# Dealing the residues of g by chunk over VectorE's two places, and issuing the adding transfers in the quarter unit of their squares

## The chip, the core and the metric

The kernel runs on one core of a Trainium2 chip. The metric is the device time in microseconds (us) of one execution; the median of three is given. The engines are TensorE (PE; its weight loads are shown as PEld), VectorE (DVE), ScalarE (ACT), GpSimd (POOL) and SyncE (SP). POOL and SP issue the transfers here, and the core's 16 DMA engines carry them.

## The reference

```python
qn = q / (np.linalg.norm(q, axis=1, keepdims=True) + 1e-06)   # q, k, v: (4, 6080, 256) float32
kn = k / (np.linalg.norm(k, axis=1, keepdims=True) + 1e-06)
s = kn.transpose(0, 2, 1) @ qn / tau                          # 256 x 256 for each of 4 batches
a = np.exp(s - s.max(-1, keepdims=True)); a /= a.sum(-1, keepdims=True) + 1e-09
x = (v @ a).reshape(24320, 256)
h = x @ w_in                                                  # 256 x 2048
g = np.where(h > 0.0, h, np.exp(np.minimum(h, 0.0)) - 1.0)
return g @ w_out                                              # 2048 x 256
```

A channel attention over tokens is followed by a feed-forward layer with ELU. Everything is float32. To keep its accuracy on TensorE, a number is split into a high part, rounded to the shorter type fp32r, and a residue, the rest of it, also in fp32r; one product is then three matmuls (high by high, high by residue, residue by high).

## The kernel before

The attention matrix of a batch is multiplied into w_in first, so that for each batch a 256 x 2048 matrix stands for both. Tokens are dealt into 48 chunks of 512 or 496, 12 to a batch. The first batch is computed in plain steps, up to about 592 us of the profile. The other 36 chunks are computed in 18 pairs, and a pair in 8 units (4 quarters fq of the 2048 columns, by j = 0 and 1): 144 units, numbered u from 0. A unit computes a 2 x 2 block of h (two chunks x = 0 and 1, two rows of columns, row = 0 and 1) with seven products in place of eight (the scheme of Strassen and Winograd), each of three matmuls (L1146, into bank_a, bank_e and bank_b), and sums of them on VectorE (L1576, L1591). The four results go through ELU: ScalarE relu and exp (L1220, L1221), VectorE the maximum (`largest`, L1224) into a tile e (named held or other). I call these four by row and chunk: e11 is row 0, x 0; e12 row 0, x 1; e21 row 1, x 0; e22 row 1, x 1.

Each e is then split. `hi_part` lets POOL issue a transfer (L1238) that rounds e into a tile of high parts (t or g), in the unit of its own. `lo_parts` subtracts it from e on VectorE in the next unit (L1245, out is a tile of residues g); it is called at two places of that unit, `before[0]` (behind L1576) and `before[1]` (behind the maximum of e21). The products with w_out (L1156 to L1158, into po) take row 1 in the second half of the next unit, x 0 ahead of x 1, and row 0 in the first half of the unit after it. In most units POOL issues the parts in the order e11, e21, e22, e12. In the unit with fq = 0 and j = 1 of every pair but the first, called the turn (u = 9, 17, 25, ...), ScalarE copies out finished sums first, and the order is e11, e21, e12, e22.

Beside the units, other work is dealt in by a planner. A task has an engine, a cost, tasks it waits for, and a due time or a level; `spend(engine, budget, now)` is called at fixed places of a unit, and writes there what is ready. Time is counted in quarters of a unit (`now = 4 * u`, and up to `now + 3`). What is written sets each engine's order, and engines then run through their orders with semaphores; the planner's times are no clock. In levels below 2 any ready task may go; in 2 and 3 only the first of the queue.

The tasks of `plan_rows` prepare the attention of the next batch (2 and then 3) from 24 groups of rows of q and k. For a group: SP loads q and k into a raw tile (`load`, L1364); POOL rounds them straight from memory (`hi`, L1375; ScalarE does it for the last group, L1373); VectorE makes the residues (`lo`, L1351); ScalarE squares the raw tile in place (L1381); POOL adds the squares into acc by an accumulating transfer (`add`, L1384). There are two raw tiles, so the load of group g waits for the adds of group g - 2. A number `late` is the count of quarters that must lie between a task and those it waits for on other engines. After the last group `plan_soft` follows (norms, softmax, transposes), and `plan_s` makes the seven matrices of the products for the next batch.

Of the kernel before, what the change touches and what calls it, by code (L numbers as in the profile page):

```python
# [54 lines left out]
def channel_attention_then_elu_ffn(ctx: ExitStack, tc, q, k, vT, tau, w_in, w_out, outT):  # L55
# [905 lines left out]
    done = []  # L961
# [5 lines left out]
    ACT, DVE, POOL, PE, SP = "act", "dve", "pool", "pe", "sp"  # L967
# [90 lines left out]
    def columns(p):  # L1058
        return span(NB + 2 * p)[1:]
# [47 lines left out]
    x = s1 - 13  # L1107
# [129 lines left out]
        else:  # L1237
            nc.gpsimd.dma_start(hi, e)  # L1238

    def lo_parts(u, row):  # L1240
        n = columns(units[u][0])[1]
        for x in range(2):
            quads[u, row, x].append(lo_ring.pop(0))
            e, hi, lo = (y[:, 0:n] for y in quads[u, row, x])
            nc.vector.tensor_sub(lo, e, hi.bitcast(F32))  # L1245
            e_ring.append(quads[u, row, x][0])
# [82 lines left out]
    def plan_rows(b, t):  # L1329

        prior = state["s_prior"]
        last_gram = None
        slots = {}
        added = {}

        def raw_of(g, y):
            x = (2 * g + y) % 4
            if x not in slots:
                room = work.tile([P, 2, 2, C], F32, tag="raw", bufs=5, name=f"raw_{b}_{x}")
                slots.update({x: room[:, 0], x + 1: room[:, 1], ("tile", x): room})  # L1340
            return slots[x]

        for g in range(NG):
            n = min(2, RP - 2 * g)
            before = state["gram_tasks"][-2 * KT : -KT][-1:] if g >= 2 else [prior.get("lo" if g else "lo before")]
            done, ready, squares = [], [], []

            def lo(g=g):
                hl = state[b, "hl", g]
                raw = slots["tile", 2 * g % 4]  # L1350
                nc.vector.tensor_sub(hl[:, 1], raw, hl[:, 0].bitcast(F32))  # L1351

            def new_hl(g=g):
                state[b, "hl", g] = work.tile([P, 2, 2, 2, C], F32R, tag="qk", bufs=3, name="qk")

            for y in range(2):
                src = (q, k)[y][b]
                rows_of = src[0 : RP * P, :].rearrange("(p r) c -> p r c", r=RP)[:, 2 * g : 2 * g + n, :]

                def load(g=g, n=n, y=y, src=src, rows_of=rows_of):  # L1360
                    raw = raw_of(g, y)
                    if n < 2:
                        nc.gpsimd.memset(raw[:, 1, :], 0.0)
                    nc.sync.dma_start(raw[:, 0:n, :], rows_of)  # L1364
                    if n < 2:
                        nc.sync.dma_start(raw[0:LEFT, 1, :], src[RP * P : N, :])

                def hi(g=g, n=n, y=y, rows_of=rows_of, new_hl=new_hl):
                    if y == 0:
                        new_hl()  # L1370
                    to = state[b, "hl", g][:, 0, y]
                    if n < 2:
                        nc.scalar.copy(to, raw_of(g, y))  # L1373
                    else:
                        nc.gpsimd.dma_start(to, rows_of)  # L1375

                def square(g=g, y=y):
                    if g == 0 and y == 0:
                        state[b, "acc"] = new_acc(b)
                    raw = raw_of(g, y)  # L1380
                    nc.scalar.activation(raw if g else state[b, "acc"][:, y], raw, AF.Square)  # L1381

                def add(g=g, y=y):
                    nc.gpsimd.dma_start(state[b, "acc"][:, y], raw_of(g, y), accum_op=ALU.add)  # L1384

                when = t + PACE * g + y * PACE / 2
                x = task(SP, 0, load, [added[g - 2, y]] if g >= 2 else [prior.get("lo")], when=when, level=2, late=2 if n == 2 else 4)
                if n == 2:
                    h = task(POOL, 0.55, hi, [*before, *done], when=when, level=2, late=1)
                else:  # L1390
                    h = task(ACT, 0.57, hi, [x, *before, *done], when=when, due=t + 16 + 5 * g, late=3)
                done = [h]
                ready += [h, x]
                squares.append((square, add))

            los = [task(DVE, 1.22, lo, ready, due=t + 4 + 4.8 * g, late=3 if n == 2 else 0)]
            for y, (square, add) in enumerate(squares):
                s = task(ACT, 0.57, square, [*los, *([] if g else [prior.get("pw")])], due=t + 4 + 4.8 * g, late=0)
                added[g, y] = task(POOL, 0.55, add, [s, *([(added[g - 1, y], 3)] if g else [])], level=1, late=1) if g else s

            for ct in range(KT):

                def items(g=g, ct=ct):
                    if g == 0 and ct == 0:
                        state[b, "gram"] = ps.tile([P, KT, C], F32, tag="gram", bufs=KT, name=f"gram_{b}")
                    return gram_items(state[b, "hl", g], state[b, "gram"], ct, g == 0, g == NG - 1)

                last_gram = task(PE, 0, items, los, level=2, late=1)
                state["gram_tasks"].append(last_gram)
        return last_gram, [added[NG - 1, y] for y in range(2)]  # L1410
# [142 lines left out]
    before = None  # L1553
    for u, (p, fq, j) in enumerate(units):
        now = PERIOD * u
        c = NB + 2 * p
        b = c // NB
        n = span(c)[2]
        more_room(u)
        if (fq, j) == (0, 0):  # L1560
            plan_pair(p)
        spend(SP, 1, now)
        assert (b, fq) in s_ready, (b, fq, u)
        va, vb, ve, vp = (x[:, 0:n] for x in (bank_a, bank_b, bank_e, p7))

        turn = u > 1 and (fq, j) == (0, 1)
        product(bank_a, p, fq, j, "A11", "B11", True)
        nc.scalar.copy(vb, va)  # L1568
        used = spend(DVE, 2.7, now)
        spend(POOL, 3.9, now)  # L1570
        product(bank_e, p, fq, j, "S3", "T3", True)
        nc.scalar.copy(vp, ve)
        multiply_out(1, now)
        spend(ACT, -0.3 if turn else 1.1, now)
        product(bank_b, p, fq, j, "S2", "T2")
        nc.vector.tensor_add(ve, vb, vp)  # L1576
        if before is not None:
            before[0]()
        product(bank_a, p, fq, j, "A12", "B21")
        e11 = new_quad(u, 0, 0)  # L1580
        relu_exp(e11, va)
        multiply_out(1, now + 1)
        spend(SP, 1, now + 1)
        product(bank_e, p, fq, j, "A22", "T4")
        e21 = new_quad(u, 1, 0)
        relu_exp(e21, ve)
        spend(ACT, -0.3, now + 1)
        largest(e11, va)
        hi_part(u, 0, 0)
        product(bank_b, p, fq, j, "S1", "T1")  # L1590
        nc.vector.tensor_add(vp, vb, vp)  # L1591
        multiply_out(2, now + 1)
        spend(ACT, -0.3 if turn else 0.3, now + 2)
        if not turn:
            e22 = new_quad(u, 1, 1)
            relu_exp(e22, vp)
        largest(e21, ve)
        hi_part(u, 1, 0)
        if before is not None:
            before[1]()  # L1600
        product(bank_b, p, fq, j, "S4", "B22")
        e12 = new_quad(u, 0, 1)
        relu_exp(e12, vb)
        if turn:
            e22 = new_quad(u, 1, 1)
            relu_exp(e22, vp)
        multiply_out(2, now + 2)
        if not turn:
            largest(e22, vp)
            hi_part(u, 1, 1)  # L1610
        multiply_out(2, now + 3)
        largest(e12, vb)
        hi_part(u, 0, 1)
        if turn:
            largest(e22, vp)
            hi_part(u, 1, 1)
        spend(POOL, 4.5, now + 3)
        spend(SP, 1, now + 3)
        used += spend(DVE, min(0.3, 3.0 - used), now + 3)
        spend(ACT, 0.6 if turn else 1.7, now + 3)  # L1620

        before = (lambda u=u: lo_parts(u, 1), lambda u=u: lo_parts(u, 0))

        for row in (1, 0):
            for x in range(2):
                for dt in range(DT):
                    outs.append(
                        (
                            c + x,
                            4 * fq + (1 - row) * 2 + j,  # L1630
                            (u, row, x),
                            dt,
                            (fq, j, row) == (0, 0, 1),
                            (fq, j, row) == (FQ - 1, 1, 0),
                        )
                    )

    now = PERIOD * len(units)
# [41 lines left out]
```

## Time and profile before

| | |
|---|---|
| median of 3 runs | 2103.23 us (2102.28 to 2105.74) |
| the profiled execution | 2105.84 us, span 2104.1 us |
| TensorE clock granted | 1.00 |
| PE, PEld busy | 2076.5 us (99%), 1836.6 us (87%) |
| DVE, ACT, POOL busy | 1589.7 us (76%), 1445.4 us (69%), 484.9 us (23%) |
| DMA | 349.29 MB, mean 166 GB/s |

The span is that of the instructions; the execution's own time is 1.7 us longer. A row of the timeline reads: start, duration, engine, line, operation, out<-in, count, and in brackets the idle time of the engine before it with what ended it. A row of the waits reads: engine and line, what it waited for, us in total, times, longest. DMA issues show as DMA_DIRECT2D on POOL, and on SPq, SyncE's queue.

### The profile page before, as it was taken

How to read it: one execution, taken by the hardware profiler on the slowest of the kernel's cores; microseconds unless marked ns; L12 is line 12 of the kernel's file. 1: busy time of each engine (PE TensorE's matmuls, PEld its weight loads, DVE VectorE, ACT ScalarE, POOL GpSimd, SP SyncE). 2: the span in 40 equal slices, each digit the busy share in tenths (PEclk: the TensorE clock that was granted, in tenths of full speed). 3: DMA queues.
4: the chain of work that ended last, by engine and by line, in shares of the span. 5: the costliest groups of instructions: out<-in, count | busy, mean ns of one | idle time of the engine just before them, and what ended most of it. 6: DMA issues, size and time to landing. Idle time of an engine off the chain costs nothing.

```text
span 2104.1 us, 29468 instructions
## 1 busy us (share of the span) xinstructions
PE 2076.5 (99%) x10009; PEld 1836.6 (87%) x10009; DVE 1589.7 (76%) x2498; ACT 1445.4 (69%) x2428; POOL 484.9 (23%) x853
## 2 busy tenths in 40 slices
PE   9999999999999999999999999999999999999998
PEld 8888888899888888888898888888888888888898
DVE  6988777777887777678688777767878767767675
ACT  6887776677776676667666667666766666666675
POOL 0000000000024343432222343443222222222221
PEclk9999999999999999999999999999999999999999
DMA  9320222221368998964567799996565543543533
GB/s 357 121 81 21 74 77 70 65 70 58 110 192 223 263 238 248 257 175 151 171 189 222 195 258 257 244 256 179 177 189 177 172 154 117 166 155 115 166 122 112
DMA packets 179863, 349.29 MB, mean 166 GB/s; under 512 B 19584, under 2 KB 56320, under 8 KB 178176
## 3 DMA queue, kind: packets, MB, share of 16 engines
q0 software_dynamic: 120960, 228.36, 38.5%
q1 hardware_dynamic: 58608, 118.91, 16.8%
q8 instruction: 79, 1.29, 0.3%
q14 instruction: 72, 0.59, 0.1%
q10 hardware_dynamic: 144, 0.13, 0.0%
HBM read 134.33 MB, written 31.20 MB: 79 GB/s over the span
## 4 chain that ended last, share of the span: by engine, by line
PE 90%; DMA 3%; DVE 3%; ACT 2%; issue 1%; POOL 0%; SPq 0%; DVEq 0%; POOLq 0%; ACTq 0%
PE bank_b L1146 12%; PE po L1157 11%; PE po L1158 11%; PE po L1156 11%; PE bank_e L1146 8%; PE bank_a L1146 8%; PE ph L446 4%; PE ph L444 4%; PE ph L445 4%; PE po L488 4%; PE po L486 4%; PE po L484 4%; PE gram L223 3%; PE gram L572 2%; DMA t<-other 2%
## 5 line engine op out<-in xcount | busy, mean ns | idle before, releaser
L1158 PE MATMUL po<-g,wo 128*128 128x512 f32 (+1 forms) x1158 | 437.6, 378 | 0.0
L1157 PE MATMUL po<-t,wo 128*128 128x512 f32 (+1 forms) x792 | 299.8, 379 | 0.0
L1156 PE MATMUL po<-t,wo 128*128 128x512 f32 (+1 forms) x792 | 299.0, 378 | 0.0
L1576 DVE TENSOR_TENSOR bank_e<-bank_b,p 128x512 f32<-128x512 f32 (+1 forms) x144 | 99.7, 693 | 245.8 <-PE bank_b L1146 238.7
L1158 PEld LDWEIGHTS po<-g,wo 128*128 128x128 f32 x1158 | 218.9, 189 | 28.2
L1568 ACT COPY bank_b<-bank_a 128x512 f32<-128x512 f32 (+1 forms) x144 | 81.5, 566 | 231.6 <-PE bank_a L1146 221.6
L1221 ACT ACTIVATE other<-other 128x512 f32<-128x512 f32 (+1 forms) x325 | 203.7, 627 | 10.3
L1238 POOL DMA_DIRECT2D t<-other x217 | 114.7, 529 | 414.0 <-DVE other L1224 249.2
L1146 PE MATMUL bank_b<-t,s 128*128 128x512 f32 (+1 forms) x528 | 181.6, 378 | 6.1 <-DVE p L1591 5.0
L1156 PEld LDWEIGHTS po<-t,wo 128*128 128x128 f32 x792 | 149.7, 189 | 19.4
L1157 PEld LDWEIGHTS po<-t,wo 128*128 128x128 f32 x792 | 149.8, 189 | 18.8
L115 DVE TENSOR_TENSOR g<-e,g 128x512 fp32r<-128x512 f32 (+1 forms) x192 | 130.9, 682 | 45.8 <-ACT g L114 44.4
L114 ACT CAST g<-e 128x512 fp32r<-128x512 f32 (+1 forms) x192 | 116.7, 608 | 69.4 <-DVE e L461 38.3
L1221 ACT ACTIVATE held<-held 128x512 f32<-128x512 f32 (+1 forms) x251 | 157.6, 628 | 8.0
L1245 DVE TENSOR_TENSOR g<-other,t 128x512 fp32r<-128x512 f32 (+1 forms) x217 | 144.5, 679 | 17.0 <-DMA t<-other 17.0
L223 PE MATMUL gram<-qk 128*128 128x256 f32 x576 | 157.3, 273 | 0.0
L1238 POOL DMA_DIRECT2D t<-held x179 | 94.7, 529 | 224.7 <-DVE held L1224 113.0
L488 PE MATMUL po<-g,wo 128*128 128x512 f32 (+1 forms) x378 | 142.7, 377 | 0.0
L486 PE MATMUL po<-g,wo 128*128 128x512 f32 (+1 forms) x378 | 142.6, 377 | 0.0
L484 PE MATMUL po<-g,wo 128*128 128x512 f32 (+1 forms) x378 | 142.6, 377 | 0.0
L1157 PE MATMUL po<-g,wo 128*128 128x512 f32 (+1 forms) x366 | 138.3, 378 | 0.0
L1156 PE MATMUL po<-g,wo 128*128 128x512 f32 (+1 forms) x366 | 138.1, 377 | 0.0
(282 smaller groups left out, 5503.2 us busy)
## 6 DMA issues: line engine op xcount, KB each, us to landing
t<-other POOLq DMA_DIRECT2D x144, 256.0 KB, 2.3
t<-held POOLq DMA_DIRECT2D x120, 256.0 KB, 2.4
acc<-raw POOLq DMA_DIRECT2D x92, 256.0 KB, 4.7
raw<-in_q_dram SPq DMA_DIRECT2D x76, 256.0 KB, 4.2
raw<-in_k_dram SPq DMA_DIRECT2D x76, 256.0 KB, 4.0
g<-other POOLq DMA_DIRECT2D x72, 256.0 KB, 2.5
t<-other POOLq DMA_DIRECT2D x73, 248.0 KB, 2.2
t<-held POOLq DMA_DIRECT2D x59, 248.0 KB, 2.2
```

The costliest lines, as they stand in the source:

```text
L115: nc.vector.tensor_sub(lo, src, hi.bitcast(F32))
L223: yield nc.tensor.matmul(gram[:, ct, :], hl[:, x, 1, r, cs], in_turns(hl[:, y, 0, r, :]), start=(first and ct == 0 and r == 0 and k == 0), ...
L484: nc.tensor.matmul(o, wo[:, f, 0, ds], hi, start=first(c, f), stop=False)
L486: nc.tensor.matmul(o, wo[:, f, 1, ds], hi, start=False, stop=False)
L488: nc.tensor.matmul(o, wo[:, f, 0, ds], lo, start=False, stop=last(c, f))
L1146: nc.tensor.matmul(bank[:, 0:n], w[:, x], y, start=(begin and k == 0), stop=(k == 2), skip_group_check=True)
L1156: yield nc.tensor.matmul(o, wo[:, f, 0, ds], hi, start=begin, stop=False)
L1157: yield nc.tensor.matmul(o, wo[:, f, 1, ds], hi, start=False, stop=False)
L1158: yield nc.tensor.matmul(o, wo[:, f, 0, ds], lo, start=False, stop=end)
L1221: nc.scalar.activation(e, e, AF.Exp, scale=-1.0)
L1238: nc.gpsimd.dma_start(hi, e)
L1245: nc.vector.tensor_sub(lo, e, hi.bitcast(F32))
```

## The change

There are three parts. First, `lo_parts` is called by chunk in place of by row: at `before[0]` VectorE now makes the residues of e21 and e11, at `before[1]` those of e22 and e12. Second, the `add` tasks get level 3 in place of 1 (behind the other tasks of POOL, and in their order), `late` 0 in place of 1, and the first call of `spend` for POOL in a unit stands behind that for ScalarE; an add can so be written in the quarter of its squares. Third, ScalarE's `hi` of the last group waits 5 quarters after its load in place of 3.

```diff
-    def lo_parts(u, row):
+    def lo_parts(u, x):
         n = columns(units[u][0])[1]
-        for x in range(2):
+        for row in (1, 0):
             quads[u, row, x].append(lo_ring.pop(0))
...
-                    h = task(ACT, 0.57, hi, [x, *before, *done], when=when, due=t + 16 + 5 * g, late=3)
+                    h = task(ACT, 0.57, hi, [x, *before, *done], when=when, due=t + 16 + 5 * g, late=5)
...
-                added[g, y] = task(POOL, 0.55, add, [s, *([(added[g - 1, y], 3)] if g else [])], level=1, late=1) if g else s
+                added[g, y] = task(POOL, 0.55, add, [s, *([(added[g - 1, y], 3)] if g else [])], level=3, late=0) if g else s
...
         used = spend(DVE, 2.7, now)
-        spend(POOL, 3.9, now)
         product(bank_e, p, fq, j, "S3", "T3", True)
         nc.scalar.copy(vp, ve)
         multiply_out(1, now)
         spend(ACT, -0.3 if turn else 1.1, now)
+        spend(POOL, 3.9, now)
...
-        before = (lambda u=u: lo_parts(u, 1), lambda u=u: lo_parts(u, 0))
+        before = (lambda u=u: lo_parts(u, 0), lambda u=u: lo_parts(u, 1))
```

VectorE in unit 98, the one behind the turn of unit 97, before. The two L1245 under L1576 are e21 and e22, the two further down e11 and e12.

```order
L1576 TENSOR_TENSOR bank_e<-bank_b,p_5100 128x512 [waits PE_49,Activation_49]
L1245 TENSOR_TENSOR g_5108<-held,g_5177 128x512 [waits DMASW4_49]
L1245 TENSOR_TENSOR g_5108<-other_5102,t_5107 128x512 [waits DMASW6_49]
L1224 SCALAR_TENSOR_TENSOR other_5103<-other_5103,bank_a 128x512 [waits Activation_49]
L1591 TENSOR_TENSOR p_5100<-bank_b,p_5100 128x512 [waits DVE_49,PE_49]
L1224 SCALAR_TENSOR_TENSOR held<-held,bank_e 128x512 [waits Activation_49]
L1245 TENSOR_TENSOR g_5108<-other_5104,g_5177 128x512 [waits DMASW3_49]
L1245 TENSOR_TENSOR g_5108<-held,t_5107 128x512 [waits DMASW5_49,PE_49]
```

The same place now: e21 and e11, and further down e22 and e12.

```order
L1576 TENSOR_TENSOR bank_e<-bank_b,p_5100 128x512 [waits PE_49,Activation_49]
L1245 TENSOR_TENSOR g_5108<-held,g_5177 128x512 [waits DMASW6_49,DVE_49]
L1245 TENSOR_TENSOR g_5108<-other_5104,g_5177 128x512 [waits DMASW5_49,DVE_49]
L1224 SCALAR_TENSOR_TENSOR other_5103<-other_5103,bank_a 128x512 [waits Activation_49]
L1591 TENSOR_TENSOR p_5100<-bank_b,p_5100 128x512 [waits DVE_49,PE_49]
L1224 SCALAR_TENSOR_TENSOR held<-held,bank_e 128x512 [waits Activation_49]
L1245 TENSOR_TENSOR g_5108<-held,t_5107 128x512 [waits DMASW0_49]
L1245 TENSOR_TENSOR g_5108<-other_5102,t_5107 128x512 [waits DMASW7_49,PE_49]
```

Of e22, whose transfer the turn issues last, the subtraction has moved from ahead of L1224 and L1591 to behind them; the count is the same.

POOL from unit 10 into unit 11, before (L1084 are parts of the next pair, from v).

```order
L1084 DMA t_5047<-in_v_dram 128x512 [waits DMAHW4_49,DMAHW3_49,DMASW6_49]
L1238 DMA t_5107<-other_5104 128x512 [waits DMASW7_49,DVE_49,PE_49]
L1238 DMA t_5107<-held 128x512 [waits DMASW0_49,DVE_49,PE_49]
L1238 DMA g_5177<-other_5103 128x512 [waits DMASW1_49,DMASW3_49,DVE_49,PE_49]
L1238 DMA t_5107<-held 128x512 [waits DMASW2_49,DMASW5_49,DVE_49,PE_49]
L1084 DMA s_5105<-in_v_dram 128x512
L1084 DMA t_5047<-in_v_dram 128x512 [waits DMASW4_49]
L1384 DMA acc_5268<-raw_2_5205 128x512 [waits Activation_49]
L1384 DMA acc_5268<-raw_2_5205 128x512 [waits DMASW6_49,Activation_49]
L1375 DMA qk<-in_q_dram 128x512 [waits DMASW7_49]
L1375 DMA qk<-in_k_dram 128x512 [waits DMASW0_49]
```

The same place now.

```order
L1084 DMA t_5047<-in_v_dram 128x512 [waits DMASW5_49]
L1384 DMA acc_5267<-raw_0_5109 128x512 [waits DMASW7_49,DMASW6_49,Activation_49]
L1384 DMA acc_5267<-raw_0_5109 128x512 [waits DMASW0_49,Activation_49]
L1238 DMA t_5107<-other_5103 128x512 [waits DVE_49,PE_49]
L1238 DMA t_5107<-held 128x512 [waits DMASW1_49,DVE_49,PE_49]
L1238 DMA g_5177<-other_5104 128x512 [waits DMASW2_49,DVE_49,PE_49]
L1238 DMA t_5107<-held 128x512 [waits DMASW3_49,DMASW4_49,DVE_49,PE_49]
L1084 DMA t_more<-in_v_dram 128x512
L1084 DMA s_4976<-in_v_dram 128x512 [waits DMASW5_49]
L1375 DMA qk<-in_q_dram 128x512 [waits DMASW6_49]
L1375 DMA qk<-in_k_dram 128x512 [waits DMASW7_49]
```

The two adds of group 7 stand ahead of the unit's four high parts now, and stood behind them. The loads of later groups, which wait for the adds, are written two to four quarters earlier for most groups of batch 2, and the whole preparation of batch 3 starts and ends about two units earlier.

ScalarE at the last group of batch 2, before: the two rounding copies L1373 stand in units 28 and 29, between the relu and exp of e21 and those of e22. Here the second, of k:

```order
L1220 ACTIVATE held<-bank_e 128x512 [waits DMASW2_49,DVE_49,PE_49]
L1221 ACTIVATE held<-held 128x512 [waits Activation_49]
L1373 CAST qk<-raw_2_5205 128x512 [waits DMAHW6_49,DMAHW5_49,Pool_49]
L1220 ACTIVATE held<-p_5100 128x512 [waits DMASW3_49,DVE_49]
L1221 ACTIVATE held<-held 128x512 [waits Activation_49]
```

Now both stand at the start of unit 29:

```order
L1568 COPY bank_b<-bank_a 128x512 [waits DVE_49,PE_49]
L1571 COPY p_5100<-bank_e 128x512 [waits PE_49]
L1373 CAST qk<-raw_2_5205 128x512 [waits DMAHW3_49,DMASW3_49,DMAHW4_49,DMASW2_49,Pool_49]
L1373 CAST qk<-raw_2_5205 128x512 [waits DMAHW6_49,DMAHW5_49,Pool_49]
L1220 ACTIVATE other_5104<-bank_a 128x512 [waits DMASW0_49,PE_49]
```

They have moved out of the middle of a unit to its start, and the load of k that the second waits for is written a unit earlier for SP.

## The prediction

> **What bounds the kernel now.** I read the page first: busy times, and the chain of waits that ended last.
>
> ```profile
> PE 2076.5 (99%) x10009; PEld 1836.6 (87%) x10009; DVE 1589.7 (76%) x2498; ACT 1445.4 (69%) x2428; POOL 484.9 (23%) x853
> PE 90%; DMA 3%; DVE 3%; ACT 2%; issue 1%; POOL 0%; SPq 0%; DVEq 0%; POOLq 0%; ACTq 0%
> ```
>
> TensorE sets the time: the chain runs through it for 90%. The change neither adds nor removes a matmul, so it can win only what TensorE waits for. I took its waits from 640 us to the end, behind the first units:
>
> ```profile
> PE bank_b L1146 <- DVE p L1591: 9.1, 8, 1.8
> PE bank_e L1146 <- DVE bank_e L1576: 5.6, 6, 1.1
> PE bank_b L1146 <- ACT bank_b L1568: 1.7, 2, 1.2
> ```
>
> Sixteen waits, 16.4 us in all: that is the purse. Each is worth a little more than it says, which the timeline of unit 98 shows, around one of the eight waits of the first row:
>
> ```profile
> 1643.68 0.69 DVE L1224 SCALAR_TENSOR_TENSOR other<-other,p 128x512 f32<-128x512 f32 x1 [0.50 <-ACT other L1221]
> 1644.91 0.53 POOL L1238 DMA_DIRECT2D t<-other  x1 [0.66 <-PE bank_a L1146]
> 1647.05 0.68 DVE L1245 TENSOR_TENSOR g<-held,g 128x512 fp32r<-128x512 f32 x1
> 1649.62 0.38 PE L1157 MATMUL po<-t,wo 128*128 128x512 f32 x1
> 1649.84 0.38 PE L1158 MATMUL po<-g,wo 128*128 128x512 f32 x1
> 1650.11 0.69 DVE L1245 TENSOR_TENSOR g<-other,t 128x512 fp32r<-128x512 f32 x1 [2.38 <-DMA t<-other]
> 1650.72 0.68 DVE L1224 SCALAR_TENSOR_TENSOR other<-other,bank_a 128x512 f32<-128x512 f32 x1
> 1651.32 0.68 DVE L1591 TENSOR_TENSOR p<-bank_b,p 128x512 f32<-128x512 f32 x1
> 1652.06 0.48 PE L1146 MATMUL bank_b<-g,s 128*128 128x512 f32 x1 [1.84 <-DVE p L1591]
> 1652.38 0.38 PE L1146 MATMUL bank_b<-t,s 128*128 128x512 f32 x1
> ```
>
> Undisturbed matmuls start 0.22 us apart (1649.62, 1649.84). Over the wait the distance is 2.22, so 2.00 are lost where the row lists 1.84, and the second matmul behind it is another 0.10 late (0.32). Each listed wait costs 0.26 more: the three rows are worth 9.1 + 2.1 = 11.2, 5.6 + 1.6 = 7.2, and 1.7 + 0.5 = 2.2 us, together 20.6.
>
> **Part one, the residues by chunk.** The rows above name the cause of the first 11.2 us. In the turn e22 is finished and issued last (1644.91). In the next unit its subtraction is VectorE's second piece behind L1576; it stands still for 2.38 us for the landing, with the maximum (L1224) and L1591 queued behind it, and TensorE waits for L1591, which frees bank_b. After 640 us each wait for L1591 is in a unit behind a turn. The change puts e11 there, which the turn issues first, and e22 behind L1591 and the next maximum. Replayed with these durations, a step of some 0.60 us from start to start: e21 at 1647.05, e11 1647.65, the maximum of e11 1648.25, L1591 1648.85, done at 1649.53, while TensorE wants it at 1650.06 (1652.06 less 2.00). The maximum of e21 follows at 1649.5, and e22 at 1650.1, when its transfer has just landed (1650.11).
>
> What is late next is e22's residue for TensorE's own product with it. How much room that has, an ordinary unit tells (unit 11: VectorE's first piece at the second place, then TensorE's first matmul on e22's residue):
>
> ```profile
> 720.98 0.68 DVE L1245 TENSOR_TENSOR g<-other,t 128x512 fp32r<-128x512 f32 x1
> 723.20 0.38 PE L1158 MATMUL po<-g,wo 128*128 128x512 f32 x1
> ```
>
> 720.98 + 0.68 = 721.66 leaves 1.5 us. In unit 98 it would be 1650.11 + 0.69 = 1650.80 against 1650.06 + 2.38 (S4's product at 720.82 to 723.20) = 1652.44: 1.6. The four subtractions are the same in number and size, so VectorE does no more. In the other units e12 is issued last, and it stood at the second place already: nothing there waits for a later landing than before. One wait stays in part: in unit 82 e21, which keeps its place, was late as well.
>
> ```profile
> 1483.10 0.68 DVE L1245 TENSOR_TENSOR g<-held,g 128x496 fp32r<-128x496 f32 x1 [0.73 <-DMA g<-held]
> 1484.76 0.68 DVE L1245 TENSOR_TENSOR g<-other,t 128x496 fp32r<-128x496 f32 x1 [0.99 <-DMA t<-other]
> ```
>
> Without e22's 0.99 of its stall some 0.5 us remain. Part one: 11.2 - 0.5 = 10.7 us gained; if e22's landing slipped by over 1.6 us, nothing.
>
> **Part two, the adds.** The second row, waits for L1576 at the head of a unit, comes from the loads of rows. Unit 12:
>
> ```profile
> 715.59 1.86 POOL L1384 DMA_DIRECT2D acc<-raw  x2
> 720.05 0.33 SPq L1364 DMA_DIRECT2D raw<-in_q_dram  x1
> 721.95 0.33 SPq L1364 DMA_DIRECT2D raw<-in_k_dram  x1
> 726.33 1.23 DVE L1351 TENSOR_TENSOR qk<-raw,qk 128x1024 fp32r<-128x1024 f32 x1 [2.60 <-DMA raw<-in_k_dram]
> 728.68 0.69 DVE L1576 TENSOR_TENSOR bank_e<-bank_b,p 128x512 f32<-128x512 f32 x1
> 729.42 0.48 PE L1146 MATMUL bank_e<-t,s 128*128 128x512 f32 x1 [0.98 <-DVE bank_e L1576]
> 727.59 1.15 ACT L1381 ACTIVATE raw<-raw 128x512 f32<-128x512 f32 x2 [1.45 <-DVE qk L1351]
> 737.76 1.78 POOL L1384 DMA_DIRECT2D acc<-raw  x2 [0.27 <-issue]
> ```
>
> The load of k goes out when the add of two groups before has landed, and VectorE then waits 2.60 us for it with L1576 behind. The last two rows show the slack in between: the squares end at 728.74 and their adds go out at 737.76, 9.0 us later, behind the unit's four high parts. The waits for adds and for loads, and the adds' time to landing (the last figure, a median), over the run:
>
> ```profile
> SPq L1364 <- DMA acc<-raw: 450.8, 83, 24.7
> DVE qk L1351 <- DMA raw<-in_k_dram: 22.1, 15, 3.0
> acc<-raw POOLq DMA_DIRECT2D x92, 256.0 KB, 4.7
> ```
>
> SP stands for the adds nearly always, so adds up to 9 us earlier let loads go up to 9 us earlier; VectorE's piece stays in its quarter. The latest wait is 3.0 us, so a third of this is enough. By the new order the groups whose piece stands in units 12, 20, 28, 60, 68 and 76 (the six waits) have loads two to four quarters earlier; in batch 3 the places go to other groups, whose loads stand five quarters ahead. I take all six, 7.2 us; the bounds are 0 and 7.2. The added wait on POOL is the add's for its squares, with the high part of e11 queued behind. But on ScalarE the squares stand ahead of e11's relu and exp, so e11 is never ready first: cost 0, and if that cover is gone, the rival below. Behind the add on the transfers' side, e11's high part may land later: the range of its landing and the next use say how much that can take.
>
> ```profile
> DMA to landing us min/median/max: 2.2/2.3/7.1
> 720.32 0.53 POOL L1238 DMA_DIRECT2D g<-other  x1 [1.75 <-DVE other L1224]
> 729.88 0.69 DVE L1245 TENSOR_TENSOR g<-other,t 128x512 fp32r<-128x512 f32 x1
> ```
>
> e11 went out at 720.32 and would be used as the second piece behind L1576, at 729.88, or 728.6 without the wait there: 8.3 us against a landing of 2.3, 7.1 at worst. Cost 0.
>
> **Part three and what shifts.** The last row, 2.2 us, is two waits for ScalarE's copy of bank_a. One follows the rounding copy of the last group in unit 29, which stood 2.60 us for its load in mid-unit; the other follows the table loads of the norms:
>
> ```profile
> ACT qk L1373 <- DMA raw<-in_k_dram: 2.6, 1, 2.6
> 973.64 1.28 ACT L1467 ACT_TABLE_LOAD   x1
> 975.05 0.57 ACT L1568 COPY bank_b<-bank_a 128x496 f32<-128x496 f32 x1
> 1501.23 0.57 ACT L1568 COPY bank_b<-bank_a 128x496 f32<-128x496 f32 x1
> ```
>
> The copy of k moves behind its load by a unit, so the first goes. The norms of batch 2 now share a unit with their matmuls, as those of batch 3 did, where the copy at 1501.23 came with no wait of TensorE. I take 2.2 (bounds 0 and 2.2).
>
> Against this stands the cost of a new deal: batch 3 is prepared two units earlier, so pieces meet other neighbours. No row shows these meetings; the nearest are today's: 15 waits for a load of rows, of which six reach TensorE at 1.2 us each (7.2 / 6). I take two of that kind, 2.4 us, between 0 and another six (7.2).
>
> Sum: 10.7 + 7.2 + 2.2 - 2.4 = 17.7, say 18 us. The profiled execution took 2105.84 us (span 2104.1 and 1.7 around it), 2.6 above the median of the runs; 18 off it gives 2087.8, and off the median of 2103.23 it gives **2085**.
>
> **Rivals.** *The transfers are full.* In the row stages the DMA engines have little left (batch 2, batch 3, and behind them):
>
> ```profile
> 641.00:836.00 195.00, 192.65 (x973) 170.00 (x973) 145.74 (x219) 129.74 (x221) 85.22 (x138) 1.00 0.94 252
> 1138.00:1489.00 351.00, 344.41 (x1726) 303.71 (x1726) 259.50 (x393) 236.30 (x404) 141.32 (x233) 1.00 0.87 236
> 1560.00:1957.00 397.00, 393.91 (x1835) 346.14 (x1834) 299.02 (x483) 265.33 (x446) 97.78 (x185) 1.00 0.49 156
> ```
>
> At a share of 0.94 an earlier issue need not be an earlier landing: the loads would then run beside e22 and e12 at the unit's end, and the six waits stay or move. Only part one is left: 2103.2 - 10.7 = 2092.5. For it speaks the 0.94; against it, that all bytes are as before and only their order changes, and that the longest wait is a third of the time won. The Trainium skill says the same of the queues (DMA: Bandwidth & Descriptors, "Issuing engines are not separate DMA queues"): transfers of SyncE, ScalarE and GpSimd run on the same 16 engines and interleave. By it alone the sum would be part one's 10.7 us, by the rows 17.7; the share of 0.94 agrees with it, and that 0.06 is left speaks for the rows.
>
> *The wait only changes its name, no change.* e22's transfer slips by over 1.6 us in the units behind a turn, its residue misses TensorE's product, and new meetings eat the rest: about 2102. For it: landings of up to 7.1 us are seen. Against: three of the eight waits (units 98, 106, 130) are past 1560, where the share is 0.49.
>
> *Slower: POOL's order.* An add issued ahead of e11 and e21 delays their landing until it passes the 8.3 us of room; VectorE then waits at its first place in every unit that follows one with adds, 46 of them (92 adds in twos), with L1591 behind. It decides from 20.6 / 46 = 0.45 us beyond the room in each. At 0.7 us: 2103.2 - 20.6 + 32 = 2115.
>
> **How the numbers follow.** The forecast, between 2080 and 2089, has a chance of 0.58; full transfers, 2090 to 2097, 0.25; no change 0.10; slower 0.07. The runs shown differ by 0.16%, so about 0.2%, 4.2 us, can be told from no change. The first two cases are faster by more: 0.83; same 0.10; slower 0.07. If all 20.6 go it is 2082.6, and the runs shown spread by 3.5 us; the range runs from 3 under that, 2079.5, to 2097, and leaves out the last two cases.
>
> **What would show it.** Right: in the units behind turns L1245 stands no longer ahead of L1591, and TensorE's row for L1591 is under 2 us after 640; adds start within 2 us of their squares' end; L1351 waits under 6 us in all (22.1 now), and TensorE's row for L1576 is gone. Wrong: L1351's row stays near 20 (the transfers are full); waits of TensorE's po lines for L1245 (e22 too late); L1245 waiting at the first place, in many units, for e11 (POOL's order).

## The result, and the profile after

The changed kernel takes 2089.44 us (median of 4 runs, 2087.04 to 2090.54) against 2104.25 for the kernel before beside it (2102.28 to 2105.74): a ratio of 0.9929 with a 95% interval of 0.9911 to 0.9946. That is 14.8 us less, where 18 were forecast; the time is inside the stated range (2079.5 to 2097), 0.4 above the forecast's own band of 2080 to 2089. Two later sets of runs, on two chips, gave 15.8 and 16.1.

The changed kernel's page, busy times and the chain of waits:

```profile
PE 2073.5 (99%) x10009; PEld 1838.0 (88%) x10009; DVE 1591.4 (76%) x2498; ACT 1445.4 (69%) x2428; POOL 484.0 (23%) x853
PE 93%; DMA 3%; DVE 2%; ACT 1%; issue 1%; POOL 0%; DVEq 0%; POOLq 0%; ACTq 0%
```

Its waits of TensorE from 640 us on, and then those of VectorE that bear on the change:

```profile
PE bank_e L1146 <- DVE bank_e L1576: 3.3, 5, 1.2
PE pw L818 <- ACT x L838: 0.7, 1, 0.7
```

```profile
DVE qk L1351 <- DMA raw<-in_k_dram: 6.1, 5, 1.7
DVE g L1245 <- DMA t<-other: 1.4, 2, 0.9
DVE g L1245 <- DMA t<-held: 1.1, 2, 0.6
```

The counts of instructions are as before; TensorE's share of the chain has gone from 90 to 93%. Of the sixteen waits, 16.4 us, all are gone, the eight for L1591, the six for L1576 that stood there and the two copies. The five for L1576 in the list are others, at units 10, 18, 58, 66 and 74; the one of L818 (a product for the next batch's matrices, behind ScalarE's scaling) is new too. VectorE's waits for the loads of k (L1351) have gone from 22.1 us in 15 to 6.1 in 5.

Unit 98 of the changed kernel, to be laid beside the unit 98 shown in the prediction:

```profile
1632.51 0.53 POOL L1238 DMA_DIRECT2D t<-held  x1 [0.66 <-PE bank_a L1146]
1634.65 0.68 DVE L1245 TENSOR_TENSOR g<-held,g 128x512 fp32r<-128x512 f32 x1
1635.25 0.68 DVE L1245 TENSOR_TENSOR g<-other,g 128x512 fp32r<-128x512 f32 x1
1636.56 0.69 DVE L1591 TENSOR_TENSOR p<-bank_b,p 128x512 f32<-128x512 f32 x1
1637.82 0.69 DVE L1245 TENSOR_TENSOR g<-held,t 128x512 fp32r<-128x512 f32 x1
1637.44 0.38 PE L1158 MATMUL po<-g,wo 128*128 128x512 f32 x1
1637.66 0.38 PE L1146 MATMUL bank_b<-g,s 128*128 128x512 f32 x1
```

e22 still goes out last (1632.51), but its residue is now the piece at 1637.82, behind L1591, which starts at 1636.56 and ends at 1637.25. TensorE's product comes at 1637.66, 0.22 behind the matmul before it: no time is lost. From issue to use e22 now has 5.31 us, and VectorE does not wait; before, the piece came up 2.82 us behind the issue and stood 2.38.

Unit 12 of the changed kernel, the squares and their adds:

```profile
725.10 1.15 ACT L1381 ACTIVATE raw<-raw 128x512 f32<-128x512 f32 x2
726.03 0.89 POOL L1384 DMA_DIRECT2D acc<-raw  x1 [1.06 <-ACT raw L1381]
727.67 0.90 POOL L1384 DMA_DIRECT2D acc<-raw  x1 [0.75 <-DVE g L1245]
```

The squares end at 726.25 and the second add goes out 1.4 us later, not 9.0. VectorE has no wait for a load here any more.

Unit 18 of the changed kernel, one of the five new waits (SPq's L1364 is the load of k):

```profile
779.15 0.55 POOL L1375 DMA_DIRECT2D qk<-in_q_dram  x1
779.67 0.56 POOL L1375 DMA_DIRECT2D qk<-in_k_dram  x1
780.19 1.86 POOL L1384 DMA_DIRECT2D acc<-raw  x2
787.39 0.33 SPq L1364 DMA_DIRECT2D raw<-in_k_dram  x1
791.43 1.23 DVE L1351 TENSOR_TENSOR qk<-raw,qk 128x1024 fp32r<-128x1024 f32 x1 [1.39 <-DMA raw<-in_k_dram]
793.32 0.48 PE L1146 MATMUL bank_e<-s 128*128 128x512 f32 x1 [0.84 <-DVE bank_e L1576]
```

The adds go out behind two rounding transfers, the load of k behind the adds at 787.39, in the turn itself, and VectorE's piece for it stands at the head of the unit behind the turn. It waits 1.39 us, L1576 behind it, and TensorE 0.84. These adds are not early ones: they start 9.4 us behind the end of their squares, where the same place of the kernel before has 8.4. Taking squares and adds in their order, 55 of the 92 adds now start within 2 us of their squares (one did before; the median fell from 9.2 to 0.5 us), but 31 start 4 to 10.5 us behind them, and the adds ahead of all five new waits are among these (8.9 to 10.5).

### The profile page after: what moved, and what is told of

The parts are those of the page before. It is cut to its first block, busy times and chain, and to the rows that moved or that the text cites. A ratio compares the mean times of both kernels' runs of the same rounds, so it can differ in the third digit from the quotient of the medians.

```text
span 2085.3 us, 29493 instructions
## 1 busy us (share of the span) xinstructions
PE 2073.5 (99%) x10009; PEld 1838.0 (88%) x10009; DVE 1591.4 (76%) x2498; ACT 1445.4 (69%) x2428; POOL 484.0 (23%) x853
## 4 chain that ended last, share of the span: by engine, by line
PE 93%; DMA 3%; DVE 2%; ACT 1%; issue 1%; POOL 0%; DVEq 0%; POOLq 0%; ACTq 0%
PE bank_b L1146 12%; PE po L1157 11%; PE po L1158 11%; PE po L1156 11%; PE bank_e L1146 8%; PE bank_a L1146 8%; PE ph L444 4%; PE ph L445 4%; PE ph L446 4%; PE po L488 4%; PE po L484 4%; PE po L486 4%; PE gram L223 3%; PE gram L572 2%; DMA acc<-raw 1%; PE gram L203 1%
## 5 line engine op out<-in xcount | busy, mean ns | idle before, releaser
L1576 DVE TENSOR_TENSOR bank_e<-bank_b,p 128x512 f32<-128x512 f32 (+1 forms) x144 | 99.9, 694 | 252.6 <-PE bank_b L1146 246.2
L1568 ACT COPY bank_b<-bank_a 128x512 f32<-128x512 f32 (+1 forms) x144 | 81.5, 566 | 237.1 <-PE bank_a L1146 229.3
L1238 POOL DMA_DIRECT2D t<-other x198 | 105.1, 531 | 319.8 <-DVE other L1224 194.6
L1238 POOL DMA_DIRECT2D t<-held x198 | 105.3, 532 | 244.6 <-DVE held L1224 109.9
L1238 POOL DMA_DIRECT2D g<-other x126 | 66.9, 531 | 297.7 <-DVE other L1224 176.9
```

## The experiments

My theory was that the gain is the sum of the removed waits, part one about 11 us and the rows' parts (two and three) about 5, less the new waits, and that these come from adds that now stand behind the rounding transfers. The main rival for the new waits was full DMA engines. All times are medians. On the first chip (the kernel before took 2104.17 us there) ran the changed kernel, the parts alone, and the adds ahead of the rounding transfers; on the second (2100.96) the places swapped, the two versions with later residues, and the one without part three; on the third (2104.63) the changed kernel, the later residues, and the kernel without adds.

**The changed kernel again.**

> The changed kernel itself, timed on the same chip as the three runs beside it. Both theories: 14 to 16 us under the kernel before; TensorE's waits from 640 us on as in its first profile, about 3.3 us for L1576 in five units (10, 18, 58, 66, 74) and none for L1591.

2088.36 us, ratio 0.9929 (0.9917 to 0.9941), 15.8 less. On the third chip:

> The changed kernel once more, on the same chip as the run with the residue of rows later, so that the two can be compared: 0.9929 of the kernel before, as twice so far.

2088.58 us, ratio 0.9923 (0.9910 to 0.9937), 16.1 less. The gain is settled at some 15 to 16 us.

**Part one alone**, on the kernel before:

```diff
-    def lo_parts(u, row):
+    def lo_parts(u, x):
...
-        for x in range(2):
+        for row in (1, 0):
...
-        before = (lambda u=u: lo_parts(u, 1), lambda u=u: lo_parts(u, 0))
+        before = (lambda u=u: lo_parts(u, 0), lambda u=u: lo_parts(u, 1))
```

> The kernel before with the residues by chunk alone. Theory A (two causes, each removed by its own part): the waits for L1591 behind the turns go, 11 us, and the six waits for L1576 in units 12, 20, 28, 60, 68, 76 and the two for ScalarE's copy stay: 2104.2 - 11 = about 2093. Theory B (the transfer engines are the limit, and what one wait gives up another takes): under 6 us, with L1351's waits grown from 22 us. If part one brought nothing: 2104.

2093.20 us, ratio 0.9952 (0.9939 to 0.9965): 11.0 less. Its waits of TensorE, and VectorE's for k:

```profile
PE bank_e L1146 <- DVE bank_e L1576: 7.1, 7, 1.1
PE bank_b L1146 <- ACT bank_b L1568: 0.5, 1, 0.5
PE bank_b L1146 <- DVE p L1591: 0.3, 1, 0.3
DVE qk L1351 <- DMA raw<-in_k_dram: 20.7, 14, 3.0
```

The waits for L1591 fall from 9.1 us to 0.3, and what is left is unit 82, as forecast; the loads of rows are as late as ever:

```profile
1476.19 0.68 DVE L1245 TENSOR_TENSOR g<-held,g 128x496 fp32r<-128x496 f32 x1 [0.84 <-DMA g<-held]
1478.67 0.90 PE L1146 MATMUL bank_b<-g,s 128*128 128x496 f32 x3 [0.35 <-DVE p L1591]
```

**The rows' parts alone**: the changed kernel with `lo_parts` by row, as before.

```diff
-        before = (lambda u=u: lo_parts(u, 0), lambda u=u: lo_parts(u, 1))
+        before = (lambda u=u: lo_parts(u, 1), lambda u=u: lo_parts(u, 0))
...
-    def lo_parts(u, x):
+    def lo_parts(u, row):
...
-        for row in (1, 0):
+        for x in range(2):
```

> The changed kernel with the residues dealt by row again, so the adds and the last group's copy alone are changed. Theory A: 7.2 + 2.2 us gained, and the new waits for L1351 in units 10, 18, 58, 66, 74 (about 5 us) given back, in the same units in which L1591 waits for e22: about 2100, with TensorE's row for L1591 at 8 to 11 us again. Theory B: 2104 or slower.

2105.52 us, ratio 1.0005 (0.9996 to 1.0014): nothing. So -11.0 and +1.4 alone make -15.8 together; 6 us belong to neither part. Its waits:

```profile
PE bank_b L1146 <- DVE p L1591: 13.2, 7, 4.1
PE bank_e L1146 <- DVE bank_e L1576: 4.1, 5, 1.3
```

TensorE waits less behind the loads (4.1 where it was 5.6), but the waits for L1591 have grown from 9.1 to 13.2. The growth is at units 42, 50 and 90: 8.2 us there, 1.3 before. No add runs near them (the adds of batch 2 end at 925 us in this kernel, and those of batch 3 run from 1155 to 1444, while these waits end at 1054, 1138 and 1572), so it is not an add that delays e22 there. Unit 42 tells it best: e22's transfer and the residue that waits for it, in the kernel before, in this one, and in the changed one.

```profile
1044.59 0.53 POOL L1238 DMA_DIRECT2D t<-other  x1 [0.63 <-DVE other L1224]
1049.11 0.68 DVE L1245 TENSOR_TENSOR g<-other,t 128x496 fp32r<-128x496 f32 x1 [1.19 <-DMA t<-other]
```

```profile
1046.01 0.53 POOL L1238 DMA_DIRECT2D t<-other  x1 [1.80 <-issue]
1052.13 0.68 DVE L1245 TENSOR_TENSOR g<-other,t 128x496 fp32r<-128x496 f32 x1 [4.61 <-DMA t<-other]
1054.02 0.48 PE L1146 MATMUL bank_b<-s,s 128*128 128x496 f32 x1 [4.10 <-DVE p L1591]
1055.73 0.62 PE L1156 MATMUL po<-g,wo 128*128 128x496 f32 x1
```

```profile
1043.90 0.53 POOL L1238 DMA_DIRECT2D t<-other  x1 [1.80 <-issue]
1048.80 0.68 DVE L1245 TENSOR_TENSOR g<-other,t 128x496 fp32r<-128x496 f32 x1 [0.90 <-DMA t<-other]
```

With the rows' new order POOL idles 1.80 us before it issues e22 here (0.63 before), and the transfer takes 6.1 us to its use instead of 4.5. It now goes out behind two loads of v on SyncE's queue (L1068, at 1044.73 and 1045.17), ahead of which it stood before (1044.59 against 1044.86). By row that is a wait of 4.10 for TensorE. By chunk, with the same late issue, VectorE waits 0.90 at its second place and TensorE not at all: of the 3.7 us between the two waits of VectorE the place is worth 2.5, and 1.2 come from an earlier landing (4.9 us to the use). Part one thus hides a cost that the other parts make: that is the interaction. By rows it is 4.1 us of waits for L1591 and the 1.7 of the next paragraph, 5.8 of the 6. What holds POOL for the 1.80 us the profile does not name ("issue"), and it stays open.

The wait costs more than itself. Here is TensorE's granted clock of the kernel with the rows' parts alone (the third figure from the end) in the two stretches behind it; the columns are stretch, length, busy time and count of PE, PEld, DVE, ACT and POOL, clock, share of the DMA engines, GB/s:

```profile
1054.00:1058.00 4.00, 3.98 (x12) 3.37 (x13) 3.82 (x7) 2.38 (x4) 1.51 (x3) 0.63 0.40 129
1058.00:1062.00 4.00, 4.00 (x20) 3.58 (x19) 2.16 (x5) 1.72 (x3) 1.59 (x3) 0.95 0.57 153
```

Behind the wait the matmuls run at half speed for some 3 us (0.62 long and 0.41 apart, from the row at 1055.73 on), and (1 - 0.63) x 4 + (1 - 0.95) x 4 = 1.7 us go there beside the 4.10. The last section shows when this happens.

**The order of the two places**: the changed kernel with the later chunk first.

```diff
-        before = (lambda u=u: lo_parts(u, 0), lambda u=u: lo_parts(u, 1))
+        before = (lambda u=u: lo_parts(u, 1), lambda u=u: lo_parts(u, 0))
```

> The changed kernel with the two places of the residues swapped: e22 and e12, the last issued, at the first place, e21 and e11 at the second. Theory A (what stands ahead of L1591 decides): TensorE's row for L1591 after 640 us, gone in the changed kernel, is back at 13 us or more as in the kernel with rows by the new deal alone, and e12 adds waits in row stages: 2105 to 2115. Rival (the order of the two places is of no weight, the gain of part one came from other neighbours in the rings of tiles): about 2088.

2115.93 us, ratio 1.0072 (1.0059 to 1.0084): 15.0 slower than before. The largest of TensorE's waits, and of VectorE's for a transfer:

```profile
PE bank_b L1146 <- DVE p L1591: 18.9, 16, 4.0
DVE g L1245 <- DMA t<-other: 34.1, 19, 4.5
```

Dealing by chunk is not what helps, but which transfer the place ahead of L1591 waits for. With both late ones there, the waits for L1591 double. Three of them (units 42, 50, 90) bring the clock down as well. In unit 90 this is TensorE's wait:

```profile
1576.30 0.48 PE L1146 MATMUL bank_b<-t,s 128*128 128x496 f32 x1 [1.91 <-DVE p L1591]
```

And the stretch behind it:

```profile
1576.00:1580.00 4.00, 3.70 (x10) 3.10 (x11) 3.81 (x8) 2.39 (x4) 1.23 (x3) 0.60 0.92 313
```

The clock is 0.60, and 1.6 us go there; with the stretch behind it (0.97) it is 1.7, and all three take 5.1.

**The adds ahead of the rounding transfers**, still in their squares' quarter:

```diff
-                added[g, y] = task(POOL, 0.55, add, [...], level=3, late=0) if g else s
+                added[g, y] = task(POOL, 0.55, add, [...], level=1, late=0) if g else s
```

> The changed kernel with level 1 for the adds in place of 3: each task stays in its quarter, but where adds and rounding transfers of rows fall in the same quarter, the adds are issued first, as in the kernel before. Theory A: the five new waits come from adds that were put behind two rounding transfers and so landed some 3 us later; they shrink to under 1 us in all, L1351 waits under 2 us in all (6.1 in the changed kernel), and the time falls by about 4 us under the changed kernel's on this chip, to about 2085. Theory B (full transfers): the loads of rows land no earlier, or what is now behind the adds is late in their place; the time is that of the changed kernel within 1.5 us.

2087.61 us, ratio 0.9923 (0.9909 to 0.9936): 0.8 under the changed kernel, within the noise, where I had expected 4. The waits at units 10, 18 and 66 go; 58 and 74 stay and grow, from 0.93 and 0.66 us in the changed kernel on this chip to 2.09 and 1.05, so TensorE's row for L1576 falls only from 3.3 to 3.1. The timeline of unit 58 of this kernel, with the load of k, the residue that waits for it, and TensorE:

```profile
1204.16 0.33 SPq L1364 DMA_DIRECT2D raw<-in_k_dram  x1
1210.39 1.23 DVE L1351 TENSOR_TENSOR qk<-raw,qk 128x1024 fp32r<-128x1024 f32 x1 [2.64 <-DMA raw<-in_k_dram]
1212.28 0.48 PE L1146 MATMUL bank_e<-t_more,s 128*128 128x512 f32 x1 [2.09 <-DVE bank_e L1576]
```

The stretch in which the load is under way, and the one behind the wait:

```profile
1205.00:1212.00 7.00, 5.20 (x26) 4.34 (x24) 3.86 (x5) 4.29 (x8) 3.38 (x5) 1.00 1.15 379
1212.00:1216.00 4.00, 3.72 (x12) 3.08 (x13) 3.58 (x7) 2.56 (x5) 0.55 (x1) 0.64 1.04 229
```

Here the load is out 3.6 us before VectorE comes to the piece (1210.39 less 2.64) and needs 6.2 us to its use. In the same unit of the changed kernel it was out 2.5 us before (1207.12) and needed 4.2: issued 1.1 us earlier, it is there 0.9 later. The order of POOL is thus one part of the matter; at units 58 and 74 what is left agrees with the rival of full transfers. The Trainium skill says of the queues (DMA: Bandwidth & Descriptors, "Issuing engines are not separate DMA queues") that transfers of all engines interleave on the same 16; the share of 1.15 while the load is under way and the 6.2 us agree, but the changed kernel has 1.10 over the same stretch, so the share alone does not set the time. And this longer wait, too, brings the clock down, to 0.64 and 0.93 in the stretch behind: (1 - 0.64) x 4 + (1 - 0.93) x 4 = 1.7 us, more than the 0.7 that the waits give (3.3 us in 4 on this chip against 3.1 in 2, each with 0.26).

**The residue of the late groups a unit later**, on the changed kernel. The edit makes VectorE's piece of rows wait four quarters behind what it needs, not three; it moves the residues of just the five groups that now stand behind a turn, by one unit each.

```diff
-            los = [task(DVE, 1.22, lo, ready, due=t + 4 + 4.8 * g, late=3 if n == 2 else 0)]
+            los = [task(DVE, 1.22, lo, ready, due=t + 4 + 4.8 * g, late=4 if n == 2 else 0)]
```

> The changed kernel with VectorE's residue of rows held 4 quarters behind its load in place of 3. This moves that piece by one unit for five groups, those of the new waits (from units 10, 18, 58, 66, 74 to the unit after), and nearly nothing else. Theory A (these loads are issued in the turn, beside four stores, and cannot land within three quarters): L1351's waits fall from 6 us to under 1, TensorE's row for L1576 from 3.3 to under 0.5, and the time by 4 to 5 us under the changed kernel, to about 2084. Theory B (full transfer engines push the wait to the next piece): 2088 within 1.5 us, with the waits at other units.

2084.57 us, ratio 0.9920 (0.9907 to 0.9933). On the third chip, beside the changed kernel's 2088.58:

> The changed kernel with the residue of rows held 4 quarters, beside the changed kernel itself. TensorE's lost time in the profiles differs by 4.0 to 4.6 us (13.3 and 13.9 against 9.3), so by Theory A it is 4 us under the changed kernel on one chip, with a ratio of about 0.991; if only noise stood behind the earlier figures, within 1 us of it.

2084.00 us, ratio 0.9907 (0.9894 to 0.9921), 4.6 under the changed kernel: a version that beats both. Of TensorE's waits from 640 us on this is all, in the first of the two:

```profile
PE pw L818 <- ACT x L838: 1.0, 1, 1.0
```

The load of k from the turn ahead of unit 18, and the residue that it is for, in its timeline:

```profile
786.38 0.33 SPq L1364 DMA_DIRECT2D raw<-in_k_dram  x1
798.06 1.22 DVE L1351 TENSOR_TENSOR qk<-raw,qk 128x1024 fp32r<-128x1024 f32 x1
```

The load goes out at nearly the same place as in the changed kernel, 1 us earlier by the clock of the trace, but has 11.7 us until its use, where it had 4.0; nothing waits for it. Both repairs together, later residues and adds first:

> The same with the adds at level 1, issued ahead of the rounding transfers of their quarter. With the pieces a unit later the order of adds has nothing left to win: the time of the run with the later residue alone, within 1.5 us, about 2084. If the adds' order were a cause of its own, 2 us or more under it.

2084.00 us, ratio 0.9916 (0.9903 to 0.9930), 0.6 from the later residues alone on that chip: nothing is left for the adds' order to win.

**Without part three**: the changed kernel with the copies' 3 quarters.

```diff
-                    h = task(ACT, 0.57, hi, [x, *before, *done], when=when, due=t + 16 + 5 * g, late=5)
+                    h = task(ACT, 0.57, hi, [x, *before, *done], when=when, due=t + 16 + 5 * g, late=3)
```

> The changed kernel without its third part: the last group's rounding copies wait 3 quarters again, stand in the middle of units 28 and 77, and the preparation ends one unit earlier. Theory A (the loads are early enough by the adds alone): no wait of ScalarE's copy over 0.7 us, the same time as the changed kernel within 1.5 us, about 2088. Rival (the third part carries the 2.2 us that the prediction gave it): 2090 to 2091, with a wait of TensorE for ScalarE's copy of bank_a in unit 30 or 78.

2091.81 us, ratio 0.9950 (0.9937 to 0.9962), 7.2 over the kernel with later residues on the same chip. By the 4.6 that this one gains on the changed kernel (on the third chip, so two chips are mixed here), part three is worth 2.6. Its waits of TensorE:

```profile
PE bank_e L1146 <- DVE bank_e L1576: 3.1, 5, 1.4
PE pw L818 <- ACT x L838: 1.8, 2, 1.2
PE bank_b L1146 <- ACT bank_b L1568: 0.8, 2, 0.4
```

ScalarE at the first of the two waits for L1568, in the timeline of unit 33:

```profile
949.23 1.28 ACT L1467 ACT_TABLE_LOAD   x1
950.64 0.57 ACT L1568 COPY bank_b<-bank_a 128x496 f32<-128x496 f32 x1
```

ScalarE has no wait for the load in L1373 here, though part three is undone. What returns are waits behind the norms' table loads (units 33 and 81) and for the scaling. By rows, with 0.26 for each wait, the two for L1568 are worth 1.3 and the scaling another 1.4. The size was right; the way was not the load.

**The kernel before without its adding transfers.**

```diff
-                    nc.gpsimd.dma_start(state[b, "acc"][:, y], raw_of(g, y), accum_op=ALU.add)
+                    pass
```

> The kernel before with the adding transfers left out, so that acc holds the squares of the first group alone and the norms are wrong; loads wait for the squares only, and 24 MB fewer are moved. Theory A (the loads of rows are late because they wait for the adds): L1351's waits of 22 us fall under 4, TensorE's row for L1576 (5.6 us) goes, and its row for L1591 (e22 behind the turns) stays at 7 to 10: 7 to 9 us under the kernel before. Rival (the loads were late on full transfer engines alone, or waited for something else): L1351 still waits 10 us or more.

2099.04 us, ratio 0.9976 (0.9967 to 0.9985): 5.6 less; 7 to 9 were expected. Its waits of TensorE, but for one of 0.5 us for L1568:

```profile
PE bank_b L1146 <- DVE p L1591: 11.4, 7, 3.5
```

And the stretch behind the longest of them, in unit 18:

```profile
798.00:802.00 4.00, 3.40 (x20) 3.10 (x21) 3.83 (x7) 2.96 (x5) 1.58 (x3) 1.00 0.65 225
```

TensorE's row for L1576 is gone, and so is VectorE's for the loads: they were late because of the adds, though the run does not part the wait for an add from the 24 MB that the adds move. The missing 2 us are e22's, whose waits grew from 9.1 to 11.4, 3.5 of it in unit 18; the clock behind that wait stayed at 1.00 in the profiled execution.

## Why the prediction was right, and where it was off

TensorE's listed waits from 640 us on, each with the 0.26 us that the prediction adds, and what the halved clock took (1 less the granted clock, over the stretches behind long waits), worked out from one profiled execution of each kernel against the 20.6 of the kernel before:

| kernel | waits, us and count | with 0.26 each, and the clock | against 20.6 | measured |
|---|---|---|---|---|
| changed | 4.0 in 6 | 5.6 | -15.0 | -14.8 |
| part one alone | 7.9 in 9 | 10.2 | -10.4 | -11.0 |
| rows' parts alone | 17.3 in 12 | 20.4 + 1.7 | +1.5 | +1.4 |
| adds ahead of rounding | 3.9 in 3 | 4.7 + 1.7 | -14.2 | -16.6 |
| before, no adds | 11.9 in 8 | 14.0 | -6.6 | -5.6 |
| later residues, third chip | 1.4 in 2 | 1.9 | -18.7 | -20.6 |

The rule holds within 2.4 us; medians are compared with single executions here, and executions of one kernel spread by 3 to 6 us. The profiled execution of the kernel before also lost 1.9 us at L572 to a load in the first batch (0 to 0.5 in the others), which with 0.26 is 2.2 of the 2.6 by which it stood over its median. On the second chip it forecasts each kernel's gain over the kernel before 2 to 5 us too large or its loss too small (the later residues: -19.3 by rows, -16.4 measured), all on one side; the kernel before was 3.2 to 3.7 us faster there than on the others, so the reference is what differs, and no profile of it on that chip shows why.

- **Part one, 10.7.** Right: 11.0 alone. The path was as replayed (L1591 ahead of e22's piece, none of the waits left). The 0.5 of unit 82 shows alone (0.35 listed, with 0.26: 0.6) and not in the changed kernel, where no wait for L1591 is left; there the term was 11.2. The 1.6 us of room for e22 were needed, which the forecast did not know: in unit 42 of the changed kernel 0.90 are used, and in its first repeat 1.7, all of it. That this was enough is partly luck.
- **Part two, 7.2.** All six waits went. But beside part one the second and third parts together brought 4.8 us (15.8 less 11.0 on the first chip), where the prediction had 7.2 + 2.2 - 2.4 = 7.0, and without part one they brought nothing, because the waits for e22 grow at units 42, 50 and 90. The prediction counted new meetings for the loads of rows alone, not for e22. A run of part two alone was not made.
- **Part three, 2.2.** Both waits went and the size holds (2.6 by runs), but by luck: the mechanism of the first half failed. Undone, the copy does not wait for its load, because the load is already early enough by part two; the gain lies in where norms and scaling fall, and about half of it is a wait (L818) that the prediction did not have.
- **New meetings, -2.4.** The mis-sized term: six waits of 4.0 us, with 0.26 each 5.6. Taking two of six by analogy was too few. The groups could have been read from the order: five residues of rows that stand at the head of units behind a turn, three quarters behind their loads, five waits. The step that failed here is "adds up to 9 us earlier": ahead of these five waits the adds are not earlier at all, and no run makes them early, so what that alone would save stays open. Against the forecast this takes 3.2 us, and the 0.5 of unit 82 gives some back: 17.7 - 3.2 + 0.5 = 15.0.
- **The rivals.** "The transfers are full" did not decide, but what remains in units 58 and 74 agrees with it. "The wait only changes its name" fell: e22's slips stay within its room, and the new meetings took 5.6 of the 20.6. "POOL's order" fell: L1245's waits for high parts are 2.5 us in all.
- **The signs.** L1591 is under 2 us (0). The others are met in part: 55 of 92 adds start within 2 us of their squares, L1351 waits 6.1 (under 6 was the mark), and L1576's row has 3.3 us left, at other units. The last two misses are the five new waits.

## What to carry to other kernels

Of several pieces that wait for transfers, put the one whose transfer goes out last behind the instruction that frees a buffer for the bounding engine, and read the order of issue at the irregular places, not in the ordinary unit: the same deal turned round took 1.0072 of the time before, in place of 0.993. Parts of a change that make transfers earlier and parts that make room for late ones can be worth little or nothing one by one; measure them alone and together. After moving producers, list which consumers now stand next to an irregular place, and move these by one step: here that gave another 4.6 us. And look at every place that the change was to move, not at one: unit 12 alone shows early adds, unit 18 late ones.

## What was not expected of the hardware

A single wait can cost TensorE half its clock for a while. Behind a wait of 4.10 us the granted clock was 0.63 over 4 us, behind one of 2.09 it was 0.64, behind one of 1.91 still 0.60; behind the wait of 3.5 us in unit 18 of the kernel without adds it stayed at 1.00. So the length of the wait does not decide by itself.

The traces show what does. In the kernel with the late chunk first the clock falls to 0.50 at 1054.55, 1139.89 and 1576.79 us and is back at 1.00 after 3.41 us each time. The distances, 85.34 and 436.90, are 25 and 128 times 3.413: time is cut into windows of that length, and the clock changes only at their ends. The table counts for some windows how long no matmul ran in them (from start to start, less some 0.21 us for a matmul of 512 or 496 columns, half of that for 256):

| kernel, unit | listed wait | window | without matmul | clock in the next window |
|---|---|---|---|---|
| late chunk first, 50 | 4.01 | 1136.47 to 1139.89 | 3.41 | 0.50 |
| late chunk first, 42 | 3.16 | 1051.14 to 1054.55 | 2.92 | 0.50 |
| rows' parts alone, 42 | 4.10 | 1051.60 to 1055.02 | 2.52 | 0.50 |
| adds ahead of rounding, 58 | 2.09 | 1209.74 to 1213.16 | 2.26 | 0.50 |
| late chunk first, 90 | 1.91 | 1573.38 to 1576.79 | 2.17 | 0.50 |
| before, 98 | 1.84 | 1649.33 to 1652.74 | 2.12 | 1.00 |
| before without adds, 18 | 3.54 | 793.40 to 796.82, and the next | 1.84, 1.91 | 1.00 |

In all thirteen traces each window with 2.17 us or more without a matmul is followed by half the clock, and none with 2.12 or less. A wait of about 2 us that falls into one window is therefore enough, and one of 3.5 us that a window's end parts in two is not. Each time costs half of 3.41, 1.7 us. The Trainium skill (TensorE: Matmul & The Clock Gate, "What's actually happening") describes a gate that halves the clock after an idle window of about 3.4 us, in windows that run freely: the length of 3.41 and the fixed places of the windows agree with it, but the window need not be idle throughout, and there the measurement decides.

The profiled executions of the kernel before and of the changed one have no such drop before the program's end, the kernel before by 0.05 us in unit 98. Where the windows lie differs from execution to execution: in the three traces of the changed kernel one starts 3.39, 0.09 and 1.81 us behind the span's start. Other executions of the kernel before and of the changed one have granted clocks of 0.998 and 0.999, and ten of the eleven of the kernel without adds 0.997 to 0.999; that agrees with drops in them, but they have no trace. A price per microsecond of wait that was read from one execution without a drop is therefore too low for waits of 2 us and more.
